# The prologue of a fused attention and FFN kernel, rearranged: S loading, key features, the first token tile

## The chip, the cores and the metric

One core of one Trainium2 chip runs the whole program. The metric is device microseconds of that core, the median over executions. Executions are compared in rounds: each version runs on the same chip as the kernel before, in turn.

## The reference

Queries, keys and values are float32 arrays of 4 batches, 4 heads, 1088 tokens and 32 channels. A feature map makes 64 features out of two 8 x 32 matrices; attention is linear in them; the result goes through an FFN with a squared relu.

```python
def phi(x):                                   # S1, S2: (8, 32)
    a = einsum('rd,bhsd->bhsr', S1, x)
    b = einsum('rd,bhsd->bhsr', S2, x)
    return einsum('bhsi,bhsj->bhsij', a, b).reshape(..., 64)
kv  = einsum('bhsf,bhsd->bhfd', phi(k), v)
z   = sum(phi(k), axis=2)
x   = einsum('bhsf,bhfd->bhsd', phi(q), kv) / (einsum('bhsf,bhf->bhs', phi(q), z) + 1e-6)
out = square(maximum(x.reshape(4352, 128) @ w_in, 0)) @ w_out   # w_in (128, 2048), w_out (2048, 128)
```

## The kernel before

The FFN is done in 192 steps: for every chunk of 384 tokens (three tiles of 128; the last chunk of a batch has 320), 16 pairs of a first matmul (`ffn1`, f16, tile pg) and a second (`ffn2`, f32, tile po). The attention of later batches runs between these steps. Only for batch 0 is there nothing to run beside, and that is the prologue: everything ahead of the first `ffn1`. Its program order is what the argument is about; each engine takes its own instructions in this order.

```python
s_nat[0:8]  <- S1 by nc.scalar.dma_start      # at the very start
load k part 0 (nc.sync)
s_nat[8:16] <- S2 by nc.sync.dma_start
load k part 1, q part 0, v ...
a_kT(0, 0)                                    # VectorE: turn k part 0
s_T = transpose(s_nat); sk, sr built from it  # sk: key features, sr: query features
...
keep_warm(9)                                  # matmuls on zeros
a_kf(0, 0); a_fs(0, 0)                        # S times k, tiles 0, 1; ScalarE copies them out of PSUM
keep_warm(1, x0)
a_kf(0, 1); a_fs(0, 1)
a_kT(0, 1); a_kT(0, 2)
kf4 <- sk x kq                                # tiles 4 to 8, turned back by VectorE (fs4)
a_qT(0, 0, 384)
replicated(2, ...)                            # rep: sr times q, 384 columns
a_kp(0, 0); a_kp(0, 1)                        # VectorE: products = key features
fs4 = transpose(kf4); kp4 = two products
replicated(0, x0[:, 0:512])
for t in range(4): a_kv(0, t); a_z(0, t)      # TensorE: 8 small matmuls for each tile
# ... GpSimd: sq, sqn, identity ...
for t in range(4, 9): a_kv(0, t); a_z(0, t)
qb = copy(rep[2])                             # ScalarE
products(0)                                   # VectorE: rep[0] * qb -> query features
replicated(1, x0[:, 512:1024])
a_kvz(0)                                      # VectorE: turn kv and z (kvt), mask them (kvz)
products(1)
a_set(2); a_qT(0, 384, 768); a_qT(0, 768, S)
a_kvs(0); a_nd(0, 0)                          # TensorE: numerator and denominator (nd)
a_kvT(0); a_kw(0); a_qc(0, 1, psf, "po")
keep_warm(4)
a_x1(0, 0); w_cast(0, 1024, ScalarE); a_x2(0, 0)   # token scale: seven VectorE operations
a_x3(0, 0, 0, 1); a_xp(0, 0, 0, 1); a_xT(0, 0, 0, 1)   # xs, turn (xp), copy (xT) of tile 0
a_x3(0, 0, 1, 2); a_xp(0, 0, 1, 2); a_xT(0, 0, 1, 2)   # of tiles 1 and 2

ffn1(0, cols 0:128); ffn1(0, cols 128:384)    # FFN, from here in full width
ffn1(1); ffn2(0, 0:128); ffn1(2); a_qg(0, 2); ffn2(0, 128:384)
for i in range(NS + 4): ffn1(i + 3); ffn2(i); planned tasks of slot i
```

## Time and profile before

| | before |
|---|---|
| timed runs, median (lowest to highest of 3) | 193.49 us (193.23 to 193.95) |
| span of the profiled execution | 657.7 us |
| TensorE busy in it | 652.3 us |

The profiled execution was one of a slow kind, 3.4 times as long as the timed ones. The page of the kernel before, its first lines (busy time, share of the span, instructions):

```profile
span 657.7 us, 4411 instructions
## 1 busy us (share of the span) xinstructions
PE 652.3 (99%) x1538; PEld 273.7 (42%) x1538; DVE 119.7 (18%) x284; ACT 138.6 (21%) x322; POOL 86.3 (13%) x168
```

A trace at full clock came later, as the first experiment, and all comparisons below use that one: span 191.0 us, TensorE busy 183.2 us.

### The profile page before, as it was taken

To read this page: it belongs to the slowest core of one execution; us is meant where nothing else is said; L and a number is where in the kernel's file an instruction comes from. 1 tells how busy PE (TensorE), PEld (TensorE's weight loads), DVE (VectorE), ACT (ScalarE), POOL (GpSimd) and SP (SyncE) were. 2 spreads that over 40 slices of the span, in tenths; PEclk is the share of its full clock that TensorE was granted. 3 is DMA by queue.
4 is the path that set the end of the run, shared out by engine and by line. 5 is a ranking of instruction groups with operands and counts; after the bars stand their busy time and mean duration, and the time that the engine had idled before them with its cause. 6 is when DMAs were issued, how large, how long until landed. Compare 5 with 4: busy or idle time off the path is not lost.

```text
span 657.7 us, 4411 instructions
## 1 busy us (share of the span) xinstructions
PE 652.3 (99%) x1538; PEld 273.7 (42%) x1538; DVE 119.7 (18%) x284; ACT 138.6 (21%) x322; POOL 86.3 (13%) x168
## 2 busy tenths in 40 slices
PE   9999999999999999999999999999999999999997
PEld 3735333533343344333443335333343333333576
DVE  3141121121131111111040111220121111201120
ACT  2032222112222121221122121121221211211210
POOL 4011030020040101101130101101102110010000
DMA  7200200001100020010300010010010100000000
GB/s 226 74 1 0 74 1 12 1 18 40 41 18 0 0 60 0 1 30 0 80 13 5 0 25 1 0 30 1 0 30 1 25 0 0 12 0 0 13 0 10
DMA packets 29936, 13.92 MB, mean 21 GB/s; under 512 B 20186, under 2 KB 28506, under 8 KB 29914
## 3 DMA queue, kind: packets, MB, share of 16 engines
q1 hardware_dynamic: 29766, 13.58, 8.3%
q8 instruction: 12, 0.20, 0.1%
q14 instruction: 10, 0.08, 0.0%
q10 hardware_dynamic: 148, 0.07, 0.0%
HBM read 8.80 MB, written 2.23 MB: 17 GB/s over the span
## 4 chain that ended last, share of the span: by engine, by line
PE 99%; DVE 0%; ACT 0%; issue 0%
PE po L931 66%; PE pg L900 17%; PE kvp L391 2%; PE pt L948 2%; PE ndn L635 2%; PE warm L1055 2%; PE qk L562 2%; PE nd L776 1%; PE rep L1083 1%; PE qk L429 1%; PE ndn L702 1%; PE kvp L405 1%; PE qc L751 0%; PE kf L329 0%; PE ndn L548 0%; PE kvp L484 0%
## 5 line engine op out<-in xcount | busy, mean ns | idle before, releaser
L931 PE MATMUL po<-g,w_o 128*128 128x384 f32 (+3 forms) x386 | 489.2, 1408 | 0.0
L931 PEld LDWEIGHTS po<-g,w_o 128*128 128x128 f32 x386 | 167.1, 437 | 171.3 <-issue 115.3
L900 PE MATMUL pg<-xT,w_in 128*128 128x384 f16 (+2 forms) x193 | 161.7, 840 | 0.2 <-ACT xT L872 0.2
L910 ACT ACTIVATE gt<-pg 128x384 f32<-128x384 f32 (+2 forms) x136 | 64.1, 472 | 401.1 <-PE pg L900 397.5
L900 PEld LDWEIGHTS <-w_in 128*128 128x128 f16 x193 | 39.5, 205 | 126.8 <-issue 125.2
L894 ACT ACTIVATE g<-gt 128x384 f32<-128x384 f32 (+2 forms) x151 | 73.5, 497 | 50.2 <-DVE gt L912 50.1
L912 DVE TENSOR_SCALAR gt<-pg 128x384 f32<-128x384 f32 (+2 forms) x57 | 30.3, 532 | 276.1 <-PE pg L900 276.1
L921 POOL TENSOR_TENSOR g<-gt 128x384 f32<-128x384 f32 (+1 forms) x40 | 31.4, 786 | 310.0 <-ACT gt L910 310.0
L597 POOL TENSOR_TENSOR qp<-tq,bs 128x384 f32<-128x384 f32 (+1 forms) x18 | 14.2, 810 | 51.0 <-DVE bs L589 51.0
L359 POOL TENSOR_TENSOR kp<-fs 128x384 f32<-128x384 f32 x9 | 14.8, 1662 | 37.3 <-DVE fs L350 37.2
L391 PE MATMUL kvp<-kp,vn 128*32 128x64 f32 x288 | 19.1, 453 | 0.0
L391 PEld LDWEIGHTS kvp<-kp,vn 128*32 128x32 f32 x288 | 14.8, 189 | 8.9 <-issue 8.8
L948 PE MATMUL pt<-w_o,g 128*128 128x128 f32 x32 | 16.5, 672 | 0.0
L571 DVE STREAM_TRANSPOSE tq<-qk 128x384 f32<-128x384 f32 (+1 forms) x9 | 5.0, 561 | 62.7 <-PE qk L562 34.2
L736 POOL TENSOR_TENSOR bt<-s 128x384 f32<-128x384 f32 (+1 forms) x10 | 7.8, 783 | 63.3 <-DVE s L710 63.3
L948 PEld LDWEIGHTS pt<-w_o,g 128*128 128x128 f32 x32 | 13.7, 442 | 4.3 <-issue 2.7
L562 PE MATMUL qk<-qT,sw 64*32 64x192 f32 (+1 forms) x144 | 13.4, 831 | 0.0
L718 DVE TENSOR_SCALAR rs<-ndn 128x384 uint32<-128x384 uint32 (+1 forms) x9 | 4.8, 535 | 47.1 <-PE ndn L702 47.1
L1055 PE MATMUL warm<-zero 128*128 128x512 f16 x13 | 11.1, 1110 | 1.0 <-DVE s_nat L167 1.0
L977 DVE SCALAR_TENSOR_TENSOR sc<-po,bt 128x384 f32<-128x384 f32 (+1 forms) x9 | 4.8, 534 | 39.0 <-PE po L931 39.0
L417 PE MATMUL kvp<-fs 128*32 128x32 f32 x54 | 11.6, 363 | 0.0
L635 PE MATMUL ndn<-ft,kw 64*32 64x192 f32 (+1 forms) x144 | 11.4, 713 | 0.0
(147 smaller groups left out, 224.1 us busy)
## 6 DMA issues: line engine op xcount, KB each, us to landing
vn<-in_v_dram SPq DMA_DIRECT2D x32, 64.0 KB, 2.1
kn<-in_k_dram SPq DMA_DIRECT2D x3, 544.0 KB, 4.9
qn<-in_q_dram SPq DMA_DIRECT2D x3, 544.0 KB
ft<-u SPq DMA_DIRECT2D x24, 48.0 KB, 1.9
out_dram<-oT SPq DMA_DIRECT2D x24, 48.0 KB, 1.8
w_in<-in_moe_w_in_dram SPq DMA_DIRECT2D x2, 512.0 KB, 5.2
w_o<-in_moe_w_out_dram SPq DMA_DIRECT2D x2, 512.0 KB, 10.6
ft<-ft SPq DMA_DIRECT2D x12, 48.0 KB, 1.9
```

The source lines that it names most:

```text
L359: (nc.vector if g == 0 else nc.gpsimd).tensor_tensor(out=_ap(st[b, "kp2"], 0, 128, 128 * (NT * g + lo), [[64, 2 * (hi - lo)], [8, 8], [1, ...
L391: nc.tensor.matmul(st[b, "kvp"][32 * h : 32 * h + 32, 0:64], _ap(vn[b], 0, n, v0 + dv * h, [[1, 32]]), kp[0:n, at[h] : at[h] + 64], start= ...
L562: nc.tensor.matmul(qg[32 * o : 32 * o + 32, 512 * r : 512 * r + n], sw[b % 2][64 * r : 64 * r + 64, 32 * (o % 2) : 32 * (o % 2) + 32], qT[ ...
L635: nc.tensor.matmul(nd[32 * h : 32 * h + 32, 512 * g : 512 * g + n], st[b, "kw"][64 * g : 64 * g + 64, 32 * h : 32 * h + 32], st[b, ch, "ft ...
L894: nc.scalar.activation(dst, src, Square)
L900: nc.tensor.matmul(pg[:, c0:c1], w_in[:, 128 * c : 128 * c + 128], st[b, "xT"][:, 384 * ch + c0 : 384 * ch + c1],)
L910: nc.scalar.activation(gt[:, c0:c1], pg[:, c0:c1], Relu)
L912: nc.vector.tensor_scalar(out=gt[:, c0:c1], in0=pg[:, c0:c1], scalar1=0.0, scalar2=None, op0=amax)
L921: (nc.vector if on[1] == "DVE" else nc.gpsimd).tensor_tensor(out=g2[:, c0:c1], in0=gt[:, c0:c1], in1=gt[:, c0:c1], op=mult)
L931: nc.tensor.matmul(st["po", b, ch][:, c0:c1], w_o[:, 128 * c : 128 * c + 128], g2s[i][1][:, c0:c1], start=first, stop=(c == NFF - 1), skip ...
L948: nc.tensor.matmul(st["pt"][:, 0:128], g2s[i][1][:, 0:128], w_o[:, 128 * c : 128 * c + 128], start=(c == 0), stop=(c == NFF - 1),)
L1055: nc.tensor.matmul(t_[:, 0:512], zero[:, 0:128], _ap(zero, 0, 128, 0, [[0, 4], [1, 128]]))
```

## The change

The intent: start the FFN earlier. S2 is issued by ScalarE, so that SyncE is free for the larger loads; key features go straight from PSUM, shared between VectorE, ScalarE and GpSimd, which also adds those of tiles 0 to 3 (kps), so that z needs fewer matmuls; the query products, nd and a shorter token scale are done for the first 128 tokens alone, and three FFN steps run on these while the other 256 tokens follow; work that the first step does not need (qc and qg, for the queries of later chunks, and the rest of qT) moves into the FFN's start. The core of the diff, with cuts marked:

```diff
-    WARM0, WARM = 9, 4
+    WARM0, WARM1 = 8, 3
     nc.scalar.dma_start(s_nat[0:8, :], S1[:, :])
+    nc.scalar.dma_start(s_nat[8:16, :], S2[:, :])
-    nc.sync.dma_start(s_nat[8:16, :], S2[:, :])
 ... (weights in smaller pieces; kT now after s_T; epsilon tiles; nd_eps, nd_part, x_part added)
+    kfa, kfb = (psf.tile([128, 512], F32, tag="pg", name="kf") for _ in range(2))
+    kpa = kp0(kfa, 0, 0, 2, nc.vector)
+    fs = ...; nc.scalar.copy(fs[:, :], kfb[:, 0:128])
+    kpb = kp0(fs, 0, 2, 2, nc.gpsimd)
+    keep_warm(WARM1, x0)
     a_kT(0, 1)
     a_kT(0, 2)
+    for t in range(4, 8): kf0(kf4, ..., t)
+    kf0(kf8, 0, 8)
     a_qT(0, 0, 384)
+    (three kp0 products on VectorE)
+    nc.gpsimd.tensor_tensor(out=kps[:, :], in0=kpa[:, :], in1=kpb[:, :], op=add)
+    for t in range(4): a_kv(0, t)
+    replicated(2, ..., 0, 128)
+    replicated(0, x0[:, 0:512], 0, 128)
+    (z of tiles 0 to 3 from kps)
     for t in range(4, 9): a_kv(0, t); a_z(...)
-    products(0)
-    replicated(1, x0[:, 512:1024])
+    replicated(1, x0[:, 512:1024], 0, 128)
+    products(0, 0, 128)
     a_kvz(0)
-    products(1)
-    a_set(2); a_qT(0, 384, 768); a_qT(0, 768, S)
-    a_nd(0, 0); a_qc(0, 1, psf, "po"); keep_warm(WARM)
-    a_x1(0, 0); a_x2(0, 0); a_x3(0, 0, 0, 1)
+    products(1, 0, 128)
+    nd_eps(nd0, 1)
+    replicated(2 / 0 / 1, ..., 128, 384)
+    nd_part(nd0, 0, 1)
+    products(0, 128, 384); products(1, 128, 384)
+    x_part(nd0, 0, 1)
+    nd_eps(nd1, 2); nd_part(nd1, 1, 2)
     a_xp(0, 0, 0, 1); a_xT(0, 0, 0, 1)
-    a_x3(0, 0, 1, 2); a_xp(0, 0, 1, 2); a_xT(0, 0, 1, 2)
+    x_part(nd1, 1, 2)
 ...
+    first, rest = (0, 128), (128, 384)
+    for i in range(LA):
+        ffn1(i, ("ACT", "ACT"), first); square_due()
+        if i: ffn2(i - 1, first)
+    a_xp(0, 0, 1, 2); a_xT(0, 0, 1, 2)
+    a_set(2)
+    ffn1(0, ("DVE", "ACT"), rest); ffn2(LA - 1, first)
+    ffn1(1, ..., rest); ffn1(2, ..., rest)
+    a_qT(0, 384, 768); a_qT(0, 768, S)
+    ffn2(0, rest)
 ... (qc and qg in the first slot of the loop)
```

## The prediction

> **What bounds the kernel now.** I first held the page against the timed runs. The profiled execution spans 657.7 us; the timed runs have a median of 193.49 us. So the profile is of an execution 3.4 times as slow as what is scored, and I had to find what in it is stretched. The timeline of the first microseconds tells:
>
> ```profile
> 1.00 7.37 PE L1055 MATMUL warm<-zero 128*128 128x512 f16 x9 [1.00 <-DVE s_nat L167]
> 3.45 0.71 DVE L293 STREAM_TRANSPOSE kT<-kn 128x512 f32<-128x512 f32 x1 [2.48 <-DMA kn<-in_k_dram]
> 4.09 0.16 DVE L300 STREAM_TRANSPOSE s_T<-s_nat 32x32 f32<-32x32 f32 x1
> 5.69 0.58 DVE L323 STREAM_TRANSPOSE qT<-qn 128x384 f32<-128x384 f32 x1
> 9.87 0.69 DVE L370 TENSOR_TENSOR kp<-fs 128x512 f32<-128x512 f32 x1 [3.60 <-ACT fs L343]
> 11.78 0.69 DVE L370 TENSOR_TENSOR kp<-fs 128x512 f32<-128x512 f32 x1 [1.21 <-ACT fs L343]
> 12.54 0.52 DVE L1099 STREAM_TRANSPOSE fs<-kf 128x320 f32<-128x320 f32 x1
> 13.09 1.56 DVE L1105 TENSOR_TENSOR kp<-fs 128x768 f32<-128x768 f32 x2
> ```
>
> Columns are start, duration, engine, line, operation, operands, and in brackets what ended the engine's wait. The weight loads of the nine warm-up matmuls are 0.84 us apart, for 512 columns: some 610 columns per us. TensorE ran at a quarter of its rate although the page prints a clock of 1.000; the other engines look normal. So I take durations of VectorE, ScalarE, GpSimd and DMA from this trace, and divide TensorE's by about four. The chain of waits (start, length, what), which is all TensorE here, is then not the chain of a timed run:
>
> ```profile
> 17.43 0.25 PE kvp L391 x5
> ...
> 24.84 2.56 PE rep L1083 x2
> 27.40 4.90 PE nd L776 x18
> ...
> 33.13 2.52 PE qc L751 x2
> 35.65 3.36 PE warm L1055 x4
> ...
> 41.80 0.63 PE pg L900
> ```
>
> The first FFN matmul starts at 39.42 us here. The work after it, 657.7 - 39.4 = 618 us, shrinks to about 157 us at four times the rate (618/3.93); if the prologue takes some 16 us, that leaves 15 to 20 us of 193.5 unexplained (tail, launch, stalls, small matmuls that do not shrink fourfold). FFN is most of the time and the change leaves it alone. In a timed run the prologue should be a chain of VectorE, ScalarE and DMA steps with TensorE idle in between. I rebuilt it (all estimates from the durations above): last part of kp done on VectorE at 4.79 + 0.71 + 0.2 + 0.58 + 2 x 0.69 + 0.52 + 1.56 = about 9.8 us; kv sums 0.5 us after that, near 10.4; kvz 0.32 + 0.30 and the second product 0.56, to 11.8; nd about 1 us, to 12.9; then the token scale:
>
> ```profile
> 32.36 0.17 DVE L790 TENSOR_SCALAR den<-nd 128x12 f32<-128x12 f32 x1 [3.48 <-PE nd L776]
> 32.45 0.55 DVE L795 TENSOR_REDUCE mx<-nd 128x12 f32<-128x384 f32 x1
> ...
> 33.97 0.69 DVE L836 TENSOR_TENSOR xs<-nd,sc 128x128 f16<-128x128 f32 x3
> 39.10 0.27 ACT L872 COPY xT<-xp 128x128 f16<-128x128 f16 x1 [4.62 <-PE xp L863]
> ```
>
> 1.61 us from den to the first xs, 0.28 for that, 0.55 for turn and copy: first FFN matmul near 15.4 us, the other two token tiles near 16.0, a full pipeline near 17.
>
> **What the Trainium skill says.** "TensorE: Matmul & The Clock Gate", Part 1: the array runs at 1.2 or 2.4 GHz by recent activity, the recorded events are unreliable, and it "has been seen stuck at K=1/4 for 50+µs". This trace agrees and goes further: 610 columns per us over the whole 657.7 us, under a printed clock of 1.000. "SBUF — State Buffer", Who interferes with whom and Two separate sides: a VectorE operation with two SBUF inputs takes a port pair from GpSimd for its whole length. The trace agrees: the 128x384 kp product on GpSimd takes 1.02 us, but 3.04 us when it meets VectorE's own 2.14 us kp product. "PSUM — Partial Sum Buffer", The four PSUM rules: GpSimd can't read PSUM; so the change copies with ScalarE for GpSimd's share. "DMA: Bandwidth & Descriptors", Issuing engines are not separate DMA queues: a second issuer saves issue time only; the S2 issue holds SP for 0.39 us here.
>
> **The change part by part**, minus is a gain at the place named.
> 1. S by ScalarE's queue: s_T now comes ahead of kT on VectorE. Both S copies are on chip at about 3.4 us, so sk is complete near 4.2 instead of 4.76, kT near 4.6 instead of 4.16: the first kf starts about 0.25 us earlier, and SP's later loads 0.39 us earlier. But VectorE holds 5.4 us of work from here to the last kp in the change too (kT 0.71, kp 0.69, kT 0.91, qT 0.58, kp 2 x 0.69, the last 0.36), with about 1 us idle while kf and ScalarE's copy pass. Last kp: about 9.7 us against 9.8. Worth 0.1.
> 2. k features: the 0.52 transpose and one kp product leave VectorE. GpSimd gets 128x512 with broadcasts: 1.02 us at 384, so about 1.3; then sr (4 x 0.2), then kps (plain, 0.83 at 384, so 1.05). Starting near 6.1, kps is there at about 9.4. TensorE must take the two kps sums ahead of tiles 4 to 8, in order: 16 + 80 small matmuls after 9.4, against 32 after 9.8 before. At 14 ns each (17.36 to 24.6 us holds 144 of them: 50 ns, over four) that ends at 10.8 against 10.3. The 16 fewer sums save 0.2. Net loss about 0.4.
> 3. First tile alone: qp products on 128 columns, 0.29 instead of 0.56 (-0.27); nd for one tile is 4 matmuls plus 2 for epsilon instead of 12 (-0.5). But three rep matmuls of 256 columns (0.43 each) stand on TensorE between kv and nd, where one of 384 (0.64) ran beside kvz: about +0.6.
> 4. Token scale: den, mx, m, sc go; reciprocal 0.22, product 0.28, maximum 0.3, exponent 0.17, scaling 0.28: 1.25 instead of 1.89 (-0.64).
> 5. Two other tiles: their own nd, then 1.8 us of scale after the first tile's 1.25 on the same engine. Near 17 us instead of 16: +1.0. In that gap TensorE does three steps of FFN on 128 columns: 3 x (0.053 + 0.213) = 0.8 us of needed work, -0.8.
> 6. qc (0.64), qg (0.3) and two qT transposes (1.0 on VectorE) leave the prologue for the first FFN steps, where TensorE waits on its partners anyway: up to +0.9 if none hides, I take +0.3.
> 7. Four warm-up matmuls go (they filled idle time: 0), weights come in smaller pieces, in another order. w_o's first packets end near 14.3 us before, ahead of need: 0.
>
> Sum: -0.1 + 0.4 - 0.27 - 0.5 + 0.6 - 0.64 + 1.0 - 0.8 + 0.3 = about 0. I move it to -1.0 by choice: parts 2 and 5 are the least certain, both rest on my guess of full-rate TensorE costs, and the 15 to 20 us that I could not explain make it likely that the prologue is longer, hence with more to save, than I reckon. That gives 193.5 - 1.0 = 192.5 us.
>
> **Rivals.**
> (a) Kps on GpSimd becomes the bound: everything from kv on waits for kpb, sr and kps in a row, 3.2 us of one engine. For it: GpSimd's 3.04 us when the ports were held. Against it: kp's first input now lies in PSUM, so VectorE has one SBUF input. It would make the time 194 to 195.5.
> (b) The early tile fills TensorE fully, and the shorter chain counts whole: 0.27 + 0.5 + 0.64 + 0.8 and perhaps 0.5 more, about 2.5 us: 191. For it: TensorE idles in this stretch. Against it: the second part comes later by as much as VectorE's second scale.
> (c) A load is the bound: if w_o's first half, one transfer of 512 KB behind 2.1 MB, were waited for before, the split alone would bring 1 to 2 us: 191.5. The first 1,024 packets of it end near 14.3 us, my ffn2 starts at 16.5: against.
> (d) Clock: fewer warm-up matmuls, and TensorE idle long enough to fall back to half rate in the first FFN steps: 1 to 3 us slower. No view of this trace can show it.
>
> **Range and chances.** From (b) with (c), 190.5, to (a), 194.8. Two per cent is 3.9 us, a quarter of a prologue that I put at 16 us: faster 0.08, slower 0.03, within 0.89.
>
> **What would show it.** In the changed trace: sk ready before 4.4 us; kp on GpSimd about 1.3 us and kps near 9.4 us plus whatever a slow TensorE adds; nd to first xs about 1.3 us instead of 1.9; a first FFN matmul earlier than before, the rest of the columns not earlier. With TensorE slow again, both traces have the rep and kv stretches as chain, and the gain seen there won't be the timed one; at full rate, first FFN near 15 us and the 256 other columns near 17. Wrong if the prologue at full rate is far from 16 us, if the kps sums come before 9 us, or if the FFN start shows TensorE waiting for weights.

## The result, and the profile after

| | before | after |
|---|---|---|
| median of the runs of the same rounds | 193.72 us (4 runs, 193.23 to 194.33) | 202.32 us (4 runs, 201.27 to 204.0) |
| ratio, 95% interval | | 1.045 (1.036 to 1.054) |

A ratio here is the mean time of one kernel's fast runs over the mean of the other's fast runs of the same rounds, so it is not quite the ratio of the medians. The change made the kernel slower by 8.6 us, outside the predicted range on the slow side. All outputs are right.

To find where, I set the FFN's first matmuls of both full traces side by side. The gap opens early and then stands still. One mark is good for this: behind the `ffn1` of steps 0 to 7 and the `ffn2` of steps 0 to 4 TensorE takes the 24 nd matmuls of the next chunk, in both kernels, and the `ffn1` after them begins at 23.82 us before and at 32.22 us after, 8.4 us apart; at the later marks the two traces are 8.4 to 8.6 us apart, as their spans are (191.0 and 199.6). So all of the loss lies in the first 32 us, and this mark (called **the mark** below) measures every version of the prologue within one trace.

The timeline of the kernel before, at full clock (start, length, engine, line, operation, operands; in brackets the idle time before and what ended it):

```profile
4.14 0.16 DVE L300 STREAM_TRANSPOSE s_T<-s_nat 32x32 f32<-32x32 f32 x1
...
9.84 0.55 DVE L1088 TENSOR_TENSOR qp<-rep,qb 128x384 f32<-128x384 f32 x1
...
10.59 0.31 PE L405 MATMUL kvp<-kp,ones 128*32 128x64 f32 x8
...
10.96 0.32 DVE L444 STREAM_TRANSPOSE kvt<-kvp 128x128 f32<-128x128 f32 x1 [0.56 <-PE kvp L405]
...
11.82 1.56 PE L776 MATMUL nd<-kvz,qp 64*128 64x66 f32 x24
...
15.04 0.69 DVE L836 TENSOR_TENSOR xs<-nd,sc 128x128 f16<-128x128 f32 x3
...
16.22 0.22 PE L900 MATMUL pg<-xT,w_in 128*128 128x128 f16 x1
...
16.84 0.43 PE L900 MATMUL pg<-xT,w_in 128*128 128x256 f16 x2 [0.40 <-ACT xT L872]
...
22.34 1.56 PE L776 MATMUL nd<-kvz,qp 64*128 64x66 f32 x24
...
23.82 0.34 PE L900 MATMUL pg<-xT,w_in 128*128 128x384 f16 x1
```

The same steps of the kernel after:

```profile
4.80 0.20 DVE L309 STREAM_TRANSPOSE s_T<-s_nat 32x32 f32<-32x32 f32 x1 [3.83 <-DMA s_nat<-in_S_dram]
...
9.57 1.27 POOL L1164 TENSOR_TENSOR kps<-kp 128x512 f32<-128x512 f32 x1
...
14.57 0.28 PE L414 MATMUL kvp<-kp,ones 128*32 128x64 f32 x8
...
15.39 0.29 DVE L1181 TENSOR_TENSOR qp<-rep,qb 128x128 f32<-128x128 f32 x1 [2.84 <-PE rep L1171]
...
15.59 0.31 DVE L502 STREAM_TRANSPOSE kvt<-kvp 128x128 f32<-128x128 f32 x1
...
16.56 1.13 PE L1171 MATMUL rep<-qT,sr 128*128 128x256 f32 x4 [0.28 <-DVE qp L1181]
...
17.62 0.66 PE L462 MATMUL nd<-kvz,qp 64*128 64x66 f32 x8
...
19.59 0.29 DVE L493 SCALAR_TENSOR_TENSOR xs<-xf,rm 128x128 f16<-128x128 f32 x1
...
20.52 0.27 PE L958 MATMUL pg<-xT,w_in 128*128 128x128 f16 x2 [0.35 <-ACT xT L930]
...
23.01 0.27 PE L958 MATMUL pg<-xT,w_in 128*128 128x256 f16 x1 [0.46 <-ACT xT L930]
...
30.73 1.56 PE L834 MATMUL nd<-kvz,qp 64*128 64x66 f32 x24
...
32.22 0.34 PE L958 MATMUL pg<-xT,w_in 128*128 128x384 f16 x1
```

What to see: s_T starts later (4.80 against 4.14). The first query product, which starts at 9.84 before, stands on VectorE until 15.39 after, waiting 2.84 us for a rep matmul, and kvt stands behind it. The wide rep matmuls stand on TensorE ahead of nd. And the first 256-column `ffn1` comes 2.49 us behind the first `ffn1`, where before it came 0.62 us behind.

The busy time of each engine in stretches of 5 us, with the granted TensorE clock, of the kernel after and then of the kernel before:

```profile
core 0: us, PE busy (x) PEld busy (x) DVE busy (x) ACT busy (x) POOL busy (x), PEclk, DMA share, GB/s
0.00:5.00 5.00, 3.20 (x8) 1.04 (x8) 0.36 (x3) 1.48 (x2) 2.61 (x24) 1.00 0.57 164
5.00:10.00 5.00, 3.92 (x19) 2.89 (x20) 2.67 (x7) 1.64 (x8) 3.25 (x11) 0.71 0.72 172
10.00:15.00 5.00, 5.00 (x137) 4.40 (x137) 1.71 (x3) 1.27 (x8) 4.51 (x20) 0.61 0.95 310
...
20.00:25.00 5.00, 3.03 (x17) 1.87 (x18) 3.06 (x10) 2.92 (x10) 0.00 (x0) 0.92 0.29 65
25.00:30.00 5.00, 5.00 (x32) 2.46 (x31) 3.38 (x12) 2.67 (x7) 0.00 (x0) 0.74 0.02 3
```

```profile
5.00:10.00 5.00, 5.00 (x123) 3.78 (x126) 4.70 (x9) 1.87 (x9) 4.49 (x13) 1.00 0.69 188
10.00:15.00 5.00, 4.92 (x100) 3.35 (x88) 3.89 (x13) 1.59 (x3) 3.12 (x17) 1.00 0.99 288
```

A clock below 1.00 is a stretch partly at half rate: after ran at half from 7.11 to 13.93 us and from 24.17 to 27.59 us, before not at all from 6.32 us on, its last 0.4 us apart. (A trace holds no clock ahead of its first recorded change, so that the 1.00 of the first stretch covers only what lies behind 3.69 us in after.) The first half-rate period follows an idle TensorE from 4.23 to 6.03 us: eight warm-up matmuls end too early for an S that comes later.

### The profile page after: what moved, and what is told of

Its sections match the earlier page's. It is cut to its first block, busy times and chain, and to the rows that moved or that the text cites.

```text
span 199.6 us, 4422 instructions
## 1 busy us (share of the span) xinstructions
PE 188.6 (95%) x1533; PEld 114.6 (57%) x1533; DVE 116.7 (58%) x285; ACT 132.5 (66%) x333; POOL 88.9 (45%) x172
## 2 busy tenths in 40 slices
DMA packets 30097, 13.93 MB, mean 70 GB/s; under 512 B 20218, under 2 KB 28538, under 8 KB 30074
## 4 chain that ended last, share of the span: by engine, by line
PE 73%; DVE 11%; DMA 4%; POOL 3%; issue 3%; ACT 1%; SPq 0%; ACTq 0%; DVEq 0%; POOLq 0%
PE po L989 44%; PE pg L958 13%; PE kvp L400 2%; PE ndn L693 2%; PE pt L1006 2%; DMA ft<-ft 2%; DMA s_nat<-in_S_dram 2%; PE qk L620 2%; PE kf L1118 2%; POOL br L1021 1%; PE rep L1171 1%; POOL kp L368 1%; DVE fs L359 1%; DMA ft<-u 1%; DVE tq L629 1%
## 5 line engine op out<-in xcount | busy, mean ns | idle before, releaser
L989 PE MATMUL po<-g,w_o 128*128 128x384 f32 (+4 forms) x390 | 145.0, 457 | 1.0 <-ACT g L952 1.0
L968 ACT ACTIVATE gt<-pg 128x384 f32<-128x384 f32 (+3 forms) x138 | 64.2, 467 | 36.3 <-PE pg L958 35.3
L989 PEld LDWEIGHTS po<-g,w_o 128*128 128x128 f32 x390 | 66.6, 191 | 35.0 <-issue 17.1
L952 ACT ACTIVATE g<-gt 128x384 f32<-128x384 f32 (+3 forms) x154 | 75.0, 499 | 7.1 <-DVE gt L970 6.5
L958 PE MATMUL pg<-xT,w_in 128*128 128x384 f16 (+3 forms) x195 | 61.5, 316 | 1.2 <-ACT xT L930 0.8
L958 PEld LDWEIGHTS <-w_in 128*128 128x128 f16 x195 | 19.4, 99 | 22.1 <-issue 4.7
L400 PE MATMUL kvp<-kp,vn 128*32 128x64 f32 x288 | 7.2, 238 | 0.1
L400 PEld LDWEIGHTS kvp<-kp,vn 128*32 128x32 f32 x288 | 5.9, 120 | 2.0 <-PE pg L958 1.6
L368 DVE TENSOR_TENSOR kp<-fs 128x1152 f32<-128x1152 f32 x3 | 6.7, 2242 | 0.0
L1006 PE MATMUL pt<-w_o,g 128*128 128x128 f32 x32 | 5.7, 274 | 0.0
```

What stands on the lines that cost most here:

```text
L368: (nc.vector if g == 0 else nc.gpsimd).tensor_tensor(out=_ap(st[b, "kp2"], 0, 128, 128 * (NT * g + lo), [[64, 2 * (hi - lo)], [8, 8], [1, ...
L400: nc.tensor.matmul(st[b, "kvp"][32 * h : 32 * h + 32, 0:64], _ap(vn[b], 0, n, v0 + dv * h, [[1, 32]]), kp[0:n, at[h] : at[h] + 64], start= ...
L952: nc.scalar.activation(dst, src, Square)
L958: nc.tensor.matmul(pg[:, c0:c1], w_in[:, 128 * c : 128 * c + 128], st[b, "xT"][:, 384 * ch + c0 : 384 * ch + c1],)
L968: nc.scalar.activation(gt[:, c0:c1], pg[:, c0:c1], Relu)
L989: nc.tensor.matmul(st["po", b, ch][:, c0:c1], w_o[:, 128 * c : 128 * c + 128], g2s[i][:, c0:c1], start=first, stop=(c == NFF - 1), skip_gr ...
```

## The experiments

Theory after reading the traces: four causes add up (S lands later; half clock; the split of queries, nd and scale; the narrow start of the FFN). Rival: one of them, the clock, makes the others only look slow. In the edits, "after" and "before" are the two kernels of the change.

**c_before.** Before, unchanged, for a trace at full clock.

> The kernel before, unchanged, for a trace at the full TensorE clock. If TensorE follows its clock here, the span is 190 to 193 us. Theory A (late S and a clock that falls): sk is ready near 4.8 us, the first FFN matmul starts near 15 to 17 us, and the granted clock doesn't fall to half in the prologue. Rival B (the steady state got slower): the first FFN matmul starts about as late as in the changed kernel, 20.5 us, and the 8 us lie after it.

192.78 us, clock 0.999 (a single run, so its state is unknown; within the range of the other runs of before). This is the trace read above.

**e1_s_sync.** After, with S2 back on SyncE:

```diff
-    nc.scalar.dma_start(s_nat[8:16, :], S2[:, :])
     load_qk(kn[0], k, 0, 0, 512)
+    nc.sync.dma_start(s_nat[8:16, :], S2[:, :])
```

> The changed kernel with S2 loaded by the SyncE queue again, in its old place after the first half of k. In the changed kernel S2 landed 3.1 us after its issue on ScalarE's queue, at 4.7 us, and everything began 1.4 us later. Theory A: sk ready 1 us earlier or more, clock not lost before kf, 197 us or less. Rival B (what follows is to blame, not S): under 1 us gained, 201 to 203 us.

200.0 us, ratio 1.034 (1.025 to 1.042) against 1.045; one of its four runs was slow and is not in the ratio. Both expected ranges were missed: it lies between them. In its trace s_T starts at 3.85 us instead of 4.80. The chain of waits of after shows why: S2, issued by ScalarE at 1.54 us behind S1, lands 3.13 us later. The time fell by about 2 us, more than the 0.9 us of the transfer; at the mark this trace, half-clocked until 13.42 us, is only 0.5 us ahead, so I keep 0.9 as the cost and hold the rest to be the clock's scatter, which is not shown.

**e2_warm16.** After, with `WARM0` 16 instead of 8.

> The changed kernel with 16 instead of 8 warm-up matmuls at the start, which end near 6.0 us, when kf can start, if the clock rises at 3.7 us as in the trace. Theory A says that the clock at half from 7.1 to 13.9 us comes from the idle 4.2 to 6.0 us: it stays at full, the k sums end 1 to 2 us earlier and the time is 199 to 201 us. Rival B: the clock falls all the same, or its fall costs nothing: 202 us.

200.54 us, ratio 1.037 (1.032 to 1.043), one run of four slow. The first half-rate period is gone (kv sums end at 12.49 us, not 14.86); a half-rate period from 21.02 to 27.85 us, in the FFN's start, takes part of it back.

**e3_before_s_act.** Before, with only the S part of the change.

```diff
+    nc.scalar.dma_start(s_nat[8:16, :], S2[:, :])
-    nc.sync.dma_start(s_nat[8:16, :], S2[:, :])
```

> The kernel before with nothing but the S part of the change: both loads of S on ScalarE's queue, s_nat cleared ahead of zero. Theory A: s_T comes about 1 us later than before (near 4.8 us, not 4.1) and kf with it, TensorE idles after its warm-up, and the time is 194.5 to 197 us. Rival B: nothing measurable, 193.2 to 194.2 us.

193.74 us, ratio 1.002 (0.997 to 1.008): harmless there, as the rival had it. In before VectorE turns kT ahead of s_T, so a late S costs less: s_T starts at 4.38 us against 4.14. (This trace is at full clock only from 10.26 us on, so its mark, 25.64, can't be set against 23.82.) It is the S part together with the new order (s_T, then kT) that lengthens the chain: in after kT waits behind s_T until 5.19 us, in before it starts at 3.50.

**e4_fill.** After, with `WARM0` 16 and eleven more matmuls on zeros in the FFN's start.

```diff
-    WARM0, WARM1 = 8, 3
+    WARM0, WARM1 = 16, 3
+    fill = psa.tile([128, 1024], F32, tag="N", name="fill")
+    keep_warm(2, fill)      # and 1 or 2 more at five other places of the start
```

> The changed kernel with 16 warm-up matmuls at the start and 11 more on zeros in the idle places of the FFN start, so that TensorE's activity keeps the clock. In the traces, TensorE was granted half its clock for 6.8 to 10.2 us of the first 28. Theory C (the clock lost through idle TensorE is most of the loss): no half clock after 4 us and before the end, 196 to 198.5 us. Rival D (the longer chain of waits is the loss, whatever the clock): clock full, but 199.5 us or more.

198.98 us, ratio 1.024 (1.016 to 1.032), between the two expected ranges, at full clock from 3.85 us until its last 2.3 us. The kv sums end at 12.41 us and the mark comes at 29.30 instead of 32.22:

```profile
12.09 0.32 PE L414 MATMUL kvp<-kp,ones 128*32 128x64 f32 x8
...
29.30 0.34 PE L958 MATMUL pg<-xT,w_in 128*128 128x384 f16 x1
```

So the half-rate periods cost 2.9 us of the 8.4, and 5.5 us remain at full clock: the rival falls.

**e6_ffn_start.** After, with the FFN's start of before: the rest of qT, qc and qg back ahead of it, all three tiles turned first, only step 0 split.

```diff
+    a_set(2); a_qT(0, 384, 768); a_qT(0, 768, S)      # ahead of a_kvs
+    a_qc(0, 1, psf, "po")
+    a_xp(0, 0, 1, 2); a_xT(0, 0, 1, 2)
-    (three steps on 128 columns, then the rest)
+    ffn1(0, 0:128); ffn1(0, 128:384); ffn1(1); ffn2(0, 0:128); ffn1(2); a_qg(0, 2); ffn2(0, 128:384)
```

> The changed kernel with the FFN start of before: qc, qg and both q transposes ahead of it or in it as before, all three token tiles turned first, only the first step split; the short scale and the split nd stay. Theory D says that three narrow steps and the q work inside the start cost 2 to 4 us: 197.5 to 200 us, and from the first FFN matmul to the sixth full ffn2 it is about as before. Rival: under 1 us gained, 201.3 or more.

200.62 us, ratio 1.031 (1.024 to 1.038), just above the expected range. From first `ffn1` to the mark it takes 7.60 us, as before (7.60), where after took 11.70. But its first `ffn1` comes at 23.29 us, 2.8 us later than after's: it must wait for all tiles, and this trace ran at half clock until 16.15 us. The time alone would have misled me; the trace shows the part that was undone.

**e7_before_narrow.** Before, with only the FFN's start of the change.

```diff
-    a_xp(0, 0, 1, 2); a_xT(0, 0, 1, 2)                # before the FFN
+    for i in range(LA): ffn1(i, ("ACT", "ACT"), first); square_due(); if i: ffn2(i - 1, first)
+    a_xp(0, 0, 1, 2); a_xT(0, 0, 1, 2)
+    ffn1(0 to 2, rest) ...
```

> The kernel before with one thing of the change: three FFN steps on the first 128 tokens ahead of the other 256, which are turned after them. qc, qg, transposes, scale, k features, loads as before. Theory D: the FFN start gets 1 to 2.5 us longer, 194.5 to 196.5 us; if the clock also drops to half there, 197. Rival (what the prediction had: the narrow steps fill idle time): 192.5 to 193.8 us.

195.76 us, ratio 1.0075 (1.0009 to 1.014). Its start, all in full clock (timeline, TensorE only):

```profile
15.70 0.22 PE L900 MATMUL pg<-xT,w_in 128*128 128x128 f16 x1 [0.35 <-ACT xT L872]
16.26 0.22 PE L900 MATMUL pg<-xT,w_in 128*128 128x128 f16 x1 [0.34 <-issue]
...
17.50 0.28 PE L863 MATMUL xp<-iden,xs 128*128 128x128 f16 x2
...
18.24 0.27 PE L900 MATMUL pg<-xT,w_in 128*128 128x256 f16 x1 [0.46 <-ACT xT L872]
```

The other tiles' xs were ready before the first of these lines, yet their turn (xp) stands on TensorE behind the narrow steps until 17.50 us, and the narrow steps leave gaps on TensorE, in which ScalarE does their relu (0.28 us each) and square (0.31). First `ffn1` to the mark: 9.69 us instead of 7.60. The narrow start costs 2.1 us where nothing has to be waited for; it gets 0.25 of that back, since the first `ffn1` comes 0.64 us behind the first xs, not 0.89, with no other tile's xp ahead of it.

**e8_kfeat.** The first half of after (S, loads, key features) with the second half of before.

> The changed kernel's first half (S by ScalarE's queue, k features on three engines, loads in their new order) with the second half of before: products on 384 columns, one nd of three tiles, the long scale, four warm-ups, the FFN start of before. If the first half costs what the traces show to the end of the k sums (3.9 us, of which S 1.1 and the half clock some 2), 195.5 to 198 us. If the loss is all in the second half, 193 to 194.5 us.

199.72 us, ratio 1.028 (1.021 to 1.034), above both expected ranges, at half clock from 7.47 to 14.29 us. Start of the FFN to the mark 7.54 us, as before. Too much is mixed for a verdict on the key features; e13 below repeats it without S and the clock.

**e9_sum.** e6 with S2 by SyncE, `WARM0` 10 and six matmuls on zeros while the FFN waits: three of the four causes undone at once.

> The changed kernel with three things undone at once: S2 by SyncE, the FFN start of before, and TensorE kept active (10 warm-ups at the start, 6 on zeros between the first and the other token tiles). If S (1.0 us), the half clock (3 us) and the FFN start (3 us) are the loss, what is left is the k features (0.4) and the wait for the second rep matmuls (0.8): 194 to 196 us. If something unseen costs more, 197 us or more.

195.51 us, ratio 1.011 (1.003 to 1.019). Undoing three causes takes back most of it, but 2.2 us stay (193.34 us before in these rounds). At the mark 2.89 stay, step by step: +0.62 to the end of the kv sums, +0.67 to kvt, +1.17 to nd, -1.26 to the first xs, +1.68 to the first `ffn1`, which again waits for all three tiles.

**e10_repair.** e9, with kT parts 1 and 2 ahead of the first kp product, without kps, and nd of the first tile ahead of the wide rep matmuls. **e12_nd_first.** e4, with only the last of these.

```diff
+    a_kT(0, 1); a_kT(0, 2)        # e10 only: right behind a_kT(0, 0)
-    (kps)                          # e10 only
+    nd_part(nd0, 0, 1)             # both: ahead of replicated(..., 128, 384)
```

> As e9_sum, and besides: all of k turned before the first kp product on VectorE, which idles 1.06 us there in the changed kernel; no kps, each of the first four tiles summed by itself, so that nothing waits for GpSimd's addition; nd of the first tile ahead of the second rep matmuls. By the traces this takes 1.5 to 2.5 us from the way to the first FFN matmul: 192 to 194 us, at or below the kernel before. Rival: VectorE or the second tiles bind instead, and it stays at e9_sum's time within 0.7 us.

> As e4_fill (full clock), with nd of the first token tile ahead of the three rep matmuls for the other tiles, which wait 0.55 us for a product that reads the same PSUM tile and then take 1.1 us. The first FFN matmul comes 0.8 to 1.6 us earlier than e4_fill's 18.66 us. If the early tile is what sets the end: 197.5 to 198.5 us against 198.98. If the other two tiles set it (they start as late or later): 198.7 to 199.5 us, no gain.

196.18 us, ratio 1.013 (1.005 to 1.021), and 199.64 us, 1.033 (1.023 to 1.042): no gain over e9 and e4. For e10 the rival held, for e12 both expectations failed: its nd begins 1.30 us earlier than e4's, and its first `ffn1` 0.46 us later. In e10 the kv sums end earlier (10.86 us against 11.52) and nd of the first tile begins at 12.35 us, but its token scale begins only at 15.29: on VectorE it stands behind the products of the other tiles, which start at 14.61, when the wide rep matmuls have ended. The early nd lost its lead on the next engine. In e12 it is the same: nd at 14.14, the products of the other tiles at 16.40, the token scale at 17.07.

**e11_before_cold.** Before, with `WARM0, WARM = 1, 0`.

> The price of the half clock by itself: the kernel before with one warm-up matmul instead of nine at the start and none of the four before the FFN. Theory C: TensorE stays at or falls to half its clock for 7 us or more in the first 20, and the time is 195 to 198 us. Rival (in the prologue TensorE waits anyway, a slower one costs nothing): 193 to 194.5 us.

194.69 us, ratio 1.007 (0.998 to 1.016), between the two expected ranges. The trace is at full clock only from 10.71 us on, its kv sums end 1.9 us later and its mark comes 1.6 us later; the interval of the time includes no difference. The clock is a real cost in the trace and a small one in this kernel's time.

**e13_k_only.** e8 with S2 by SyncE and `WARM0` 10: the key features and the loads' order, little else.

> The version with the new k features and the old second half (199.72 us, clock at half until 14.29 us), with S2 back on SyncE and ten warm-up matmuls. What it still has of the change is the k features on three engines, the loads' order and the weights in smaller pieces. If the costs add (S about 1.0 to 1.1, clock about 3, FFN start 3, k features 0.4 to 0.5), this is 193.6 to 194.4 us, within 1% of before, first FFN near 16.5 to 17, kv sums ending near 11.4. If the k features are dearer than the sums say, so that they alone carry the 2.2 us that the sum of three repairs left over, it is 195 to 196 and the split of the second half is innocent.

A miss: 197.02 us, ratio 1.013 (1.006 to 1.020). Even its run at full clock, 196.48 us, is 2.2 us over the median of before (194.25 us). kv sums end at 12.29 us, not 11.4, and kvt begins only at 13.71. So something in this half was dearer than my sum. The traces of e9 and e13 show what, for they are alike up to the first rep matmuls: these are 128 columns wide in e9 (9.15 to 9.86 us) and 384 wide in e13 (9.23 to 10.79), they stand on TensorE ahead of the remaining sums, and these end 0.77 us later. kvt is late by the order that e15 and e16 show.

**e14_scale_ahead.** e12, with the token scale of the first tile ahead of the other tiles' products on VectorE.

```diff
+    x_part(nd0, 0, 1)
     products(0, 128, 384); products(1, 128, 384)
-    x_part(nd0, 0, 1)
```

> The version with nd of the first tile ahead of the second rep matmuls (199.64 us, no gain), and now also the first tile's token scale ahead of the other tiles' products on VectorE. Theory: the early tile did not pay because its scale stood behind those products; now the first FFN matmul comes 1.2 to 1.8 us earlier, near 17 us, but the other two tiles' scale starts later by the first tile's 1.3 us, and the narrow FFN steps wait for them, so the time stays within 0.6 us of 199.0. Rival: the early first tile is what counts, and the time falls by over 1 us, to 197.5 to 198.

199.85 us, ratio 1.026 (1.020 to 1.032), against 1.033 for e12 with overlapping intervals: both expectations missed, for the first `ffn1` came at 19.66 us, not near 17. Timeline:

```profile
16.57 0.44 DVE L493 SCALAR_TENSOR_TENSOR xs<-xf,rm 128x128 f16<-128x128 f32 x1
...
17.00 0.76 DVE L1181 TENSOR_TENSOR qp<-rep,qb 128x256 f32<-128x256 f32 x2
...
18.14 1.01 PE L462 MATMUL nd<-kvz,qp 64*128 64x66 f32 x16
...
19.07 0.23 PE L921 MATMUL xp<-iden,xs 128*128 128x128 f16 x1
```

The first tile's xs is ready at 17.01 us. Its turn starts 2.06 us later, because on TensorE nd of the other tiles stands ahead of it, and that waits for their products (its first matmuls start at 17.80 us, when these are done). Each time one queue was mended, the next queue held the tile. That TensorE does matmuls strictly in program order is what the Trainium skill says ("PSUM — Partial Sum Buffer", Engine vs sequencer instructions); these lines agree.

**e15_k_repair.** e13, with kT parts 1 and 2 ahead of the first kp product and without kps (z tile by tile).

> The k-features-only version, with parts 1 and 2 of kT ahead of the first kp product on VectorE, and without the added kps sum on GpSimd (z taken tile by tile). In the larger repair these moved the end of the kv sums from 11.45 to 10.8 us but gained no time. Theory: there the second half's split ate the gain; here, with the old second half, the 0.6 us reaches the first FFN matmul: 0.4 to 0.7 us below the k-features-only version, 192.9 to 193.8. Rival: something else than kv holds the second half (products, weights), and the two versions agree within 0.2 us.

195.57 us, ratio 1.005 (0.997 to 1.013); 194.70 and 194.94 us at clock 0.996 and 0.997, so 1.5 to 1.8 us under e13's full-clock run: a larger gain than expected, from a dearer e13, so that the level was missed. Up to nd the traces differ by 0.75 us, little more than expected; e13's is at half clock from 15.34 us on, so the rest is not located. e15's trace shows what is left (timeline, VectorE):

```profile
12.68 0.56 DVE L1180 TENSOR_TENSOR qp<-rep,qb 128x384 f32<-128x384 f32 x1 [2.67 <-PE rep L1170]
13.15 0.30 DVE L504 STREAM_TRANSPOSE kvt<-kvp 128x128 f32<-128x128 f32 x1
```

The last kv sum ended at 11.72 us, and kvt starts 1.43 us after it. In before it starts 0.06 us after.

**e16_product_first.** e15 with one pair of lines in the order of before:

```diff
-    replicated(1, x0[:, 512:1024], 0, 384)
     products(0, 0, 384)
+    replicated(1, x0[:, 512:1024], 0, 384)
```

> The k-repair version (195.57 us) with one pair of lines turned back to the order of before: the first feature product of the queries ahead of the second rep matmul, not after it. Theory: in the k-repair version that product waits 2.67 us on VectorE for the rep matmul, which stands behind all kv sums, and the turning of the kv sums (kvt) stands behind the product: kvt starts 1.5 us after the last kv sum, in before 0.1 us. With the order of before, kvt starts within 0.2 us of the last kv sum, the first FFN matmul comes about 1.2 us earlier (near 16.9), and the time falls by 1.0 to 1.3 us, to 194.2 to 194.6, level with before. Rival: the product then delays the rep matmul or the kp products on VectorE, and the time stays at 195.3 to 195.8.

The same two lines of this trace:

```profile
10.41 0.56 DVE L1180 TENSOR_TENSOR qp<-rep,qb 128x384 f32<-128x384 f32 x1 [0.37 <-PE rep L1170]
...
11.62 0.32 DVE L504 STREAM_TRANSPOSE kvt<-kvp 128x128 f32<-128x128 f32 x1 [0.66 <-PE kvp L416]
```

kvt starts 0.07 us after the last kv sum (11.55), the first `ffn1` at 16.68 us and the mark at 24.22, both 1.46 us earlier than in e15, somewhat more than expected. 193.84 us, a little below the range; ratio to before 0.992 (0.987 to 0.997). The product reads columns 0 to 383 of the PSUM tile x0, the rep matmul writes columns 512 and up of the same tile: nothing forces it to wait, except that it comes behind that matmul in program order, and the wait seems to be set for the tile as a whole. (The wide rep matmul of after at 16.56 us fits this: it writes columns below 384 and waits for a product that reads columns from 512 on.)

Is e16 better than both? Its median is 8.5 us under that of after (of other rounds). Against before it was faster in these rounds by 0.8%, but the eleven runs of before had a median of 195.45 us here, 1.7 above their first rounds, with clocks from 0.986 to 1.000; e16's six had 0.994 to 0.999. At full clock the traces say equal: mark 24.22 against 23.82, span 191.3 against 191.0. So what it wins may be no more than the clock: the five runs of before with 0.993 or more have a median of 194.09 us. That is not shown, and which of its parts would steady the clock I did not test.

**e17_first_tile.** e14, with xp of the first tile ahead of the other tiles' nd, and the product ahead of the rep matmul.

```diff
+    products(0, 0, 128)
     replicated(1, x0[:, 512:1024], 0, 128)
-    products(0, 0, 128)
+    a_xp(0, 0, 0, 1); a_xT(0, 0, 0, 1)
     nd_eps(nd1, 2); nd_part(nd1, 1, 2); a_kw(0)
-    a_xp(0, 0, 0, 1); a_xT(0, 0, 0, 1)
```

> The scale-ahead version (199.85 us, full clock), with the turn of the first tile (xp) ahead of the other tiles' nd on TensorE, and with the product ahead of the second rep matmul. In the scale-ahead version the first tile's xs was done at 17.0 us and its xp waited on TensorE until 19.07 behind nd of the other tiles, which waited for products on VectorE. Theory: the first FFN matmul now comes at 16.7 to 17.2 us, 2.5 us earlier, and the time follows only by what the other tiles gain from the product's place, 0.3 to 0.7 us: 199.1 to 199.6; the early tile itself is worth nothing, because the FFN's rate is set by when all three tiles are there. Rival, the change's own intent: half or more of the 2.5 us reaches the end, 197.4 to 198.4.

199.46 us, ratio 1.019 (1.012 to 1.027). The time fell in the range, the reason did not hold: xT of the first tile is ready at 16.94 us, but the first `ffn1` starts at 18.98, since `ffn1` itself is still behind the other tiles' nd on TensorE (17.28 to 18.62 us), and behind two of the experiment's own matmuls on zeros (from 18.54 us, 0.4 us of TensorE). The mark comes at 29.63 us, 0.67 earlier than in e14 although the kv sums end 0.41 later; 0.68 of these 1.08 us is kvt, which is no longer late. An FFN start at 17 us was never reached, so what such a start would be worth stays open.

**e18_before_order.** Before, with the same pair of lines in the order of the change.

> The kernel before with that one pair of lines in the order of the change: second rep matmul ahead of the first product. Theory: the product then waits behind all kv sums, kvt starts after it, about 1.2 to 1.4 us after the last kv sum instead of 0.1 us, and the whole kernel is 1.0 to 1.4 us slower, 194.8 to 195.6 at a before of 193.7 to 194.2. Rival: the 0.5 us of the product fit into the wait for kv, and the time is within 0.3 us of before.

Inconclusive in time: 195.65 us, ratio 1.002 (0.996 to 1.007), in the noisy rounds of e16; the rival's number came out, but the interval reaches up to +0.7%, which is the 1.4 us of the theory. In the trace the mechanism is there: the last kv sum ends at 10.33 us, kvt starts at 11.75, 1.42 us later. But that execution had its kv sums 0.57 us earlier than the trace of before, and half clock from 14.01 to 17.42 us, so its mark (25.57) cannot be set against 23.82. Ahead of that period nd starts 0.81 us later than in before, in spite of the earlier sums: 1.38 us in all. To the mark, the cost of the order is shown at full clock by e15 and e16 alone.

## Why the prediction was wrong, point by point

The path from S to the mark, in microseconds from the start, out of the traces; the last column is the difference between e4 (the change at full clock) and before:

| | before | after | e4 (full clock) | e16 | e4 less before, step by step |
|---|---|---|---|---|---|
| last kv sum ends | 10.90 | 14.86 | 12.41 | 11.55 | +1.51 |
| kvt starts | 10.96 | 15.59 | 13.15 | 11.62 | +0.68 |
| nd of the first tile starts | 11.82 | 17.62 | 15.44 | 12.54 | +1.43 |
| first xs ends | 15.33 | 19.88 | 18.02 | 16.04 | -0.93 |
| first `ffn1` | 16.22 | 20.52 | 18.66 | 16.68 | -0.25 |
| the mark | 23.82 | 32.22 | 29.30 | 24.22 | +3.04 |

The steps add up to 5.48 us; the clock adds 2.92 (after's mark less e4's); together 8.40. Two of e4's steps hold a collision that after does not have: kvz took 0.57 us and the first xs 0.62, each while GpSimd cast a part of w_in (13.36 to 13.97 and 17.27 to 17.88 us); in after they took 0.30 and 0.29. In e9, which has neither, these two steps are +1.17 and -1.26. This is how the prediction's terms fared:

- **S** was put at -0.1 and is +0.9 (kv sums end at 12.41 us in e4 and at 11.52 in e9, which differs there by S2 on SyncE and the count of warm-ups). The step that failed is "both S copies are on chip at about 3.4 us": S2 landed at 4.67. That SyncE's later loads are issued earlier was right, and won nothing on this path.
- **Key features** at +0.4 are +0.6 (11.52 in e9 less 10.90): right, and in the mechanism too. As predicted, the last 96 sums stand in a row behind kps: in e9 kps ends at 9.85 us and the sums run from 9.90 to 11.52, 16.9 ns each instead of 14. What failed is VectorE's last kp "about 9.7 us against 9.8": it ends at 10.69 in e9 and at 9.93 in before. The list of VectorE's work there adds up to 4.63 us, not 5.4, and the engine stands idle for 2.2 us, not 1. The GpSimd product took 1.06 us and the sum 1.27, against 1.3 and 1.05. Rival (a) is not what happened: the rep matmuls ahead of the sums end at 9.86, so that kps alone did not hold kv. But it was not free either: with kT ahead of kp and without the sum, e15 gained 1.5 to 1.8 us on e13 in time, 0.57 at the end of the kv sums.
- **The order of product and rep matmul** was in no term. It costs 0.68 in the narrow form and 1.43 to 1.46 in the wide one. I read the diff for what it adds and removes, not for two lines that changed places.
- **Rep matmuls and the narrow product**, +0.6 - 0.27 = +0.33, are +1.43: the matmuls are 256 wide as reckoned, but two of the three wait for the products that read the same tile, so that they begin at 16.56 us in after, when kvz is done and nd could have begun. In e12, with nd ahead of them, the way from kvt to nd is 1.26 us shorter than in e4.
- **Token scale and nd of one tile** at -0.5 - 0.64 = -1.14 are -0.93 (-1.26 in e9): right, in mechanism and nearly in size.
- **The FFN's start**, +1.0 - 0.8 + 0.3 = +0.5 in the prediction, is +2.79 (3.04 less the 0.25 of the step before, which is the narrow order's too): the largest error at full clock. The credit of 0.8 assumed that three narrow steps fill a gap. But the other 256 columns now come 2.49 us behind the first `ffn1`, not 0.62, since ScalarE's relu and square pace the narrow steps and the other tiles' turn stands behind them on TensorE. e7 puts the narrow order alone at 1.84 us (2.09 - 0.25); qc, which now stands in the FFN, takes 0.81 in e4. Together 2.65 of the 2.79. That the two add up is an estimate: no run moves qc alone, and e4's own last pair of matmuls on zeros, directly ahead of a full `ffn1` at 23.50 us, may hold 0.4 of the 2.79, which would then be the clock's.
- **The clock**, rival (d), was named with 1 to 3 us and then given no weight in the sum and 0.03 of the chances. It cost 2.9 us. "They filled idle time: 0" is the step that failed: filling idle time is what those matmuls were for, and with more of them (e2, e4) the first half-rate period goes, in e4 the second too. What each period costs by itself was not measured.
- **A load** (rival (c)) is not the bound: in the traces of before and after no instruction waits for w_o.
- **The -1.0 by choice** rested on 15 to 20 us that I could not explain. They were not in the prologue, whose first `ffn1` at 16.22 us was close to the 15.4 predicted; so they lie in the steady part, which the change leaves alone; I did not trace them further.

So the sign went wrong by four mis-sized terms of the same direction (S 1.0, rep and order 1.8, FFN start 2.3, clock 2.9) and one choice (1.0): 9.0 of the 9.4 us between a mark predicted 1.0 earlier and one measured 8.4 later. Rival (b), that the early tile counts whole, was never put to the test by the change, because the in-order queues of VectorE and TensorE kept the tile from starting early.

## What to carry to other kernels

Splitting off a first tile can pay only if its instructions come ahead of the other tiles' on every engine that it crosses (that it pays then was not shown here); check each queue in turn, because the lead won on one is lost on the next. In a diff, look for pairs of lines that changed places as closely as for lines added: one pair cost 1.46 us here, and turning it back repaired most of the 1.86 us at the mark that were left. Warm-up matmuls belong to the wait that they cover, so a change that moves the wait has to move them too; and judge a prologue by one mark in a full-clock trace, since the time alone mixes it with the clock.

## What the Trainium skill lacked or had wrong

- "TensorE: Matmul & The Clock Gate", Part 1: its table says that the clock falls after at least one idle window of about 3.4 us. The periods here do change in steps of 3.41 us, which agrees; but after fell to half with an idle stretch of 1.80 us (4.23 to 6.03), and e13 with one of 1.62 us (13.13 to 14.75, half from 15.34). So less than a whole idle window is enough, as a later passage of that part on short idles between matmuls has it too; the page lacks how busy a window has to be.
- The same part has the array stuck at quarter rate for "50+µs"; the first profile here shows it over a whole execution of 657.7 us, under a printed clock of 1.000.
- "DMA: Bandwidth & Descriptors", Issuing engines are not separate DMA queues: a second issuer saves issue time only. That holds for SyncE here, but the page lacks the other side: the second copy issued by ScalarE came up behind the first one's issue (0.59 us), landed 3.13 us after its own, and made s_T start at 4.80 us instead of 3.85.
- I found on none of the pages that a VectorE product can be held by a matmul into other columns of the same PSUM tile, here for 2.67 us (e15) against 0.37 (e16), with 1.46 us at the mark. Whether the chip or the program's own waits ask for it, these runs do not show.
